# Retention and a mixture of adapters: all attention in 64-token steps on four 64x64 array tiles, in a fixed order

## The chip, the cores and the metric

The kernel runs on one core of a Trainium2 chip. The metric is the device time of one execution in microseconds, as the median of several runs; lower is better. The engines are named as in the profile: PE is TensorE (matmuls), PEld its weight loads, DVE VectorE, ACT ScalarE, POOL GpSimd, SP SyncE (here only a queue that issues DMAs). A line number such as L291 is a line of the kernel before; lines of the kernel after are given where a step has no counterpart.

## The reference

Eight batches of eight heads, 576 tokens, 64 values a head. Scores q k^T are scaled, multiplied by a causal decay gamma_h^(i-j), and applied to v. The result, 512 values a token, goes through a mixture of adapters: eight gates, the best two by a softmax, each adapter of rank 16, and the input added.

```python
scores = scale * np.matmul(q, k.transpose(0, 1, 3, 2))
gamma = 1.0 - 2.0 ** (-5.0 - np.arange(H, dtype=np.float32))
Dmat = np.where(rel >= 0, gamma[:, None, None] ** rel[None, :, :], 0.0)
ret = scores * Dmat[None, :, :, :]
x = np.matmul(ret, v)                       # then as (tokens, 512)
logits = x @ w_gate                         # 8 gates, best 2, softmax weights w
delta[mask] += w[mask, k, None] * ((x[mask] @ A[e]) @ B[e])
out = x + delta
```

All inputs and outputs are fp32.

## The kernel before, in words

**Tiling.** The 576 tokens are four chunks of 128 and a half chunk of 64. A unit is one chunk of two batches (a pair); there are 16 full units and four half units (64 tokens of two batches, stacked on the 128 partitions). Loads go by quads: one chunk of four batches, 1 MB each for q, k and v, into three rotating buffers a tensor; a quad serves two units. The first quad is loaded in two halves.

**The decay** is split: gamma^i goes into q when its transpose is evicted (L241, with aqp), gamma^-j into v on POOL (L197, in place). What earlier chunks contribute is a state P a head and pair, 64x64: chunk by chunk k^T v is added (L387) and POOL multiplies the sum by gamma^128 (L388).

**Stages of one unit.** T (L229): PE transposes q and k, 128x64 outputs; DVE evicts q (L241), ACT k (L250). S (L291): scores, 16 matmuls with 64 rows, 128 stationary columns and 128 moving columns; DVE masks them with the triangle into rt (L302). O: the state part P^T q into px (L359, 16 matmuls on 64x64 tiles with 128 columns, from chunk 1 on) and the state update k^T v into pu (L373, 16). R (L408): the masked part, v^T rt, 16 matmuls with 128 rows, accumulated on px; ACT copies px to xT (L417). Z (L447): xT against adapters A and gates, 128x136 columns; the routing on DVE and ACT (lg L460, m L462, ns L463, sg L468, cm L473, zc L479). B (L512): xT transposed back into po; X (L493): zc transposed, zT by ACT (L498); Y (L533): zT against B, added in po; ACT copies po to osb (L543); a store of each batch on SP (L548). An fp32 matmul is recorded as two passes, each with a weight load.

**The order** is written as a loop over units, one unit after the other, with the next unit's transposes and the previous unit's Y inside it (lines 561 to 576); the framework's scheduler may still move instructions. Eight PSUM banks rotate under one tag. A quad's loads are issued two quads ahead (L562). Half units use 64x64 tiles for scores (L291 with 64 columns, four tiles), the state part (L341, two tiles) and the masked part (L426).

```python
for t in range(NU):
    if t % 2 == 0:
        issue(t // 2 + 2)
    stage_S(t)
    ...
    stage_O(t)
    stage_R(t)
    ...
    stage_T(t + 1)
    stage_B(t - 1); stage_X(t - 1)
    stage_Z(t)
    stage_Y(t - 1)
```

Of the kernel before, what the change touches and what calls it, by code (L numbers as in the profile page):

```python
# [14 lines left out]
AFT = mybir.ActivationFunctionType  # L15


@with_exitstack
def kernel(
# [10 lines left out]
    nc = tc.nc  # L30
# [6 lines left out]
    NP = B // 2  # L37
    NFULL = S // 128
    LH = S - 128 * NFULL
    QUAD = 4  # L40
    NQ = B // QUAD

    scale = 1.0 / float(np.sqrt(Dh))
    gam = 1.0 - 2.0 ** (-5.0 - np.arange(H, dtype=np.float64))
    jj = np.arange(128, dtype=np.float64)

    ident32_np = np.eye(128, dtype=np.float32)
    tri_np = (jj[None, :] >= jj[:, None]).astype(np.float32)
    j64 = np.arange(128) % 64
    i64 = np.arange(64)  # L50
    trih_np = (i64[None, :] >= j64[:, None]).astype(np.float32)
    aqp_np = np.zeros((128, HP, 128), dtype=np.float32)
    g128_np = np.zeros((128, HP), dtype=np.float32)
    for hp in range(HP):
        for ho in range(2):
            g = gam[2 * hp + ho]
            aqp_np[64 * ho : 64 * ho + 64, hp, :] = scale * g ** jj[None, :]
            g128_np[64 * ho : 64 * ho + 64, hp] = g**128.0
    gv_np = np.stack([gam[h] ** (-jj) for h in range(H)], axis=1).astype(np.float32)
    gvh_np = np.stack([gam[h] ** (-j64.astype(np.float64)) for h in range(H)], axis=1).astype(  # L60
        np.float32
    )
    i64_np = np.concatenate([np.eye(64), np.eye(64)], axis=0).astype(np.float32)
    first_np = i64_np
    rest_np = np.concatenate(
        [ident32_np, tri_np, trih_np, gv_np, gvh_np, g128_np], axis=1
    ).astype(np.float32)
    NPK = rest_np.shape[1]
    dr_first = nc.inline_tensor(first_np, "c_first")
    dr_rest = nc.inline_tensor(rest_np, "c_rest")  # L70
    dr_aqp = nc.inline_tensor(aqp_np, "c_aqp")
# [4 lines left out]
    mo = ctx.enter_context(tc.tile_pool(name="moe", bufs=3))  # L76
    pp = ctx.enter_context(tc.tile_pool(name="pp", bufs=8, space=bass.MemoryType.PSUM))

    id64 = cpool.tile([128, 64], FP32, tag="id64", name="id64")
    nc.sync.dma_start(out=id64, in_=dr_first.ap())  # L80
    warm = cpool.tile([128, 1], FP32, tag="warm", name="warm")
    nc.vector.memset(warm, 0.0)
    nc.scalar.activation(out=warm, in_=warm, func=AFT.Sigmoid)
    pack = cpool.tile([128, NPK], FP32, tag="pack", name="pack")
    aqp = cpool.tile([128, HP, 128], FP32, tag="aqp", name="aqp")
    ident32 = pack[:, 0:128]
    tri = pack[:, 128:256]
    trih = pack[:, 256:320]
    gv = pack[:, 320 : 320 + H]
    gvh = pack[:, 320 + H : 320 + 2 * H]  # L90
    g128 = pack[:, 320 + 2 * H : 320 + 2 * H + HP]

    AW = []
    for par in range(2):
        AW.append(cpool.tile([128, HP, ER + E], FP32, tag=f"AW{par}", name=f"AW{par}"))
    Bcat = cpool.tile([128, Dm], FP16, tag="Bcat", name="Bcat")
    ident16 = cpool.tile([128, 128], FP16, tag="ident16", name="ident16")

    def load_moe():
        for dt in range(HP):  # L100
            nc.sync.dma_start(  # L101
                out=AW[0][:, dt, 0:ER].rearrange("p (e r) -> p e r", e=E),
                in_=moe_A[:, 128 * dt : 128 * dt + 128, :].rearrange("e d r -> d e r"),
            )
        nc.sync.dma_start(
            out=AW[0][:, :, ER : ER + E],
            in_=moe_w_gate.rearrange("(t p) e -> p t e", p=128),
        )
        nc.gpsimd.dma_start(out=Bcat, in_=moe_B.rearrange("e r d -> (e r) d"))


    nat = {}

    def issue_full(c, qd, split):
        tiles = []
        for src, tag in ((q, "q32"), (k, "k32"), (v, "v32")):
            tiles.append((src, iop.tile([128, QUAD * H, Dh], FP32, tag=tag, name=tag)))
        parts = ((0, 2), (2, 4)) if split else ((0, 4),)
        for lo, hi in parts:
            for src, tl in tiles:  # L120
                if split and lo == 0 and src is k:
                    nc.sync.dma_start(out=aqp, in_=dr_aqp.ap())
                if split and lo == 0 and src is v:
                    nc.sync.dma_start(out=pack, in_=dr_rest.ap())
                if split and lo == 2 and src is q:
                    load_moe()
                nc.sync.dma_start(  # L127
                    out=tl[:, lo * H : hi * H, :],
                    in_=src[
                        QUAD * qd + lo : QUAD * qd + hi, :, 128 * c : 128 * c + 128, :  # L130
                    ].rearrange("b h j d -> j (b h) d"),
                )
        for half in range(2):
            nat[(c, 2 * qd + half)] = [
                tl[:, half * 2 * H : half * 2 * H + 2 * H, :] for _, tl in tiles
            ]

    def issue_half(qd):

        s0 = 128 * NFULL  # L140
        tiles = []
        for src, tag in ((q, "q32"), (k, "k32"), (v, "v32")):
            tiles.append((src, iop.tile([128, QUAD * H, Dh], FP32, tag=tag, name=tag)))
        for slot in range(2):
            for src, tl in tiles:
                for par in range(2):
                    b = QUAD * qd + 2 * slot + par
                    nc.sync.dma_start(
                        out=tl[64 * par : 64 * par + LH, slot * H : slot * H + H, :],
                        in_=src[b, :, s0 : s0 + LH, :].rearrange("h j d -> j h d"),  # L150
                    )
            nat[(NFULL, 2 * qd + slot)] = [
                tl[:, slot * H : slot * H + H, :] for _, tl in tiles
            ]

    quads = [(c, qd) for c in range(NFULL + 1) for qd in range(NQ)]

    def issue(n):
        if n < len(quads):
            c, qd = quads[n]  # L160
            if c < NFULL:
                issue_full(c, qd, n == 0)
            else:
                issue_half(qd)

    issue(0)

    issue(1)
    nc.vector.tensor_copy(out=ident16, in_=ident32)
    gdec = cpool.tile([128, HP, 2, Dh], FP32, tag="gdec", name="gdec")  # L170
    nc.gpsimd.tensor_copy(
        out=gdec.rearrange("p a b d -> p a (b d)"),
        in_=g128.unsqueeze(2).broadcast_to((128, HP, 2 * Dh)),
    )
    P = [
        cpool.tile([128, HP, 2, Dh], FP32, tag=f"P{bp}", name=f"P{bp}")
        for bp in range(NP)
    ]

    def swap_aw():  # L180
        for ho in range(2):
            nc.gpsimd.tensor_copy(
                out=AW[1][64 * ho : 64 * ho + 64],
                in_=AW[0][64 - 64 * ho : 128 - 64 * ho],
            )

    units = [(c, 2 * qd + s) for c, qd in quads for s in range(2)]
    st = {}
# [131 lines left out]
    def col(full, b, ho):  # L320
        return (ho ^ b) if full else ho
# [289 lines left out]
```

## Time and profile before

| | |
|---|---|
| Median of 3 runs | 207.31 us (205.72 to 207.71) |
| Span of the profiled execution, first to last instruction | 205.1 us |
| The profiled execution's own time beyond its span | not recorded; the runs lie 0.7 to 2.7 us above the span |
| PE busy / weight loads | 183.8 us (90%) / 166.2 us (81%) |
| DVE, ACT, POOL busy | 108.7, 76.6, 59.6 us |
| HBM read, written | 29.32 MB, 9.44 MB |
| Share of the 16 DMA engines (main queue) | 68.0% |

Busy shares are averages over a start that waits for loads, a long even middle and a short tail. The granted PE clock is full from the start's end on. In the groups a line such as "x512 | 34.6, 288" gives the count, the busy microseconds together and the mean nanoseconds of one; what follows is the engine's idle time before them and what ended it. "64*128" in a matmul's row is its tile of the array, rows by columns. In the chain of waits each piece has its start, its length and what it is.

### The profile page before, as it was taken

Reading aid. Unit: us, or ns where it says so; the run is one execution under the profiler, and the core shown is the slowest. Engines: PE = TensorE matmul, PEld = TensorE weight load, DVE = VectorE, ACT = ScalarE, POOL = GpSimd, SP = SyncE. Lnnn points to the kernel's source line nnn. Section 1 sums busy time; section 2 is a strip of 40 time slices with the busy share of each in tenths; the row PEclk is TensorE's granted clock in tenths of the full one; section 3 lists DMA queues with packets and bytes.
Section 4 is the critical chain, followed back from the end, with each engine's and each line's share of the span. In section 5 each row is a group of like instructions: output and inputs, shape, how many; then the busy total and the mean of one; then the engine's idle time right before and its main releaser. Section 6 shows DMA issues by size and latency. Waiting matters only on the chain.

```text
span 205.1 us, 8039 instructions
## 1 busy us (share of the span) xinstructions
PE 183.8 (90%) x3564; PEld 166.2 (81%) x3564; DVE 108.7 (53%) x286; ACT 76.6 (37%) x206; POOL 59.6 (29%) x60
## 2 busy tenths in 40 slices
PE   0476989799999999999999999999999999999950
PEld 0376969598999999999999999999999899888830
DVE  0226364937374746465656565656565655456630
ACT  2022324153525262625252525253434344454430
POOL 1144323521818202727202720643222402000000
PEclk9999999999999999999999999999999999999997
DMA  5989999799998988991799969756545311222222
GB/s 114 277 109 246 249 243 280 194 290 290 253 319 245 261 249 274 284 297 36 220 286 254 266 215 293 213 145 179 150 118 158 96 51 60 101 79 76 58 47 61
DMA packets 57442, 39.14 MB, mean 191 GB/s; under 512 B 30912, under 2 KB 52672, under 8 KB 57408
## 3 DMA queue, kind: packets, MB, share of 16 engines
q1 hardware_dynamic: 57264, 38.50, 68.0%
q8 instruction: 28, 0.46, 0.9%
q0 software_dynamic: 144, 0.13, 0.4%
q14 instruction: 6, 0.05, 0.1%
HBM read 29.32 MB, written 9.44 MB: 189 GB/s over the span
## 4 chain that ended last, share of the span: by engine, by line
PE 72%; SPq 9%; DVE 7%; DMA 5%; ACT 3%; issue 1%; ACTq 0%
PE pz L447 16%; PE px L408 12%; PE ps_s L291 12%; PE pu L373 6%; PE px L359 6%; PE pt_q L229 5%; DMA k<-in_k_dram 5%; PE po L512 4%; SPq L127 4%; PE pt_k L229 4%; PE po L533 3%; DVE rt L302 2%; PE px L426 2%; ACT osb L543 2%; SPq L101 2%; PE pzt L493 2%
## 5 line engine op out<-in xcount | busy, mean ns | idle before, releaser
L197 POOL TENSOR_TENSOR v<-v,pack 128x512 f32<-128x512 f32 x36 | 36.6, 1042 | 28.0 <-DMA v<-in_v_dram 28.0
L417 ACT COPY xT<-px 128x512 f32<-128x512 f32 x32 | 18.7, 585 | 66.0 <-PE px L408 66.0
L388 POOL TENSOR_TENSOR P<-pn,gdec 128x512 f32<-128x512 f32 x16 | 20.3, 1271 | 75.3 <-DVE pn L387 58.9
L302 DVE TENSOR_TENSOR rt<-ps_s,pack 128x512 f32<-128x512 f32 x64 | 39.7, 682 | 4.2 <-PE ps_s L291 4.2
L291 PE MATMUL ps_s<-qT,kT 64*128 64x128 f32 (+1 forms) x640 | 37.4, 275 | 1.2 <-ACT kT L250 1.2
L447 PE MATMUL pz<-AW,xT 128*128 128x136 f32 x288 | 37.8, 283 | 0.4 <-ACT zT L498 0.4
L291 PEld LDWEIGHTS ps_s<-qT,kT 64*128 64x128 f32 (+1 forms) x640 | 33.7, 184 | 5.3 <-DVE lg L460 3.4
L241 DVE TENSOR_TENSOR qT<-pt_q,aqp 128x512 f32<-128x512 f32 x32 | 20.6, 686 | 31.1 <-PE pt_q L229 31.1
L408 PE MATMUL px<-rt,v 128*64 128x128 f32 x512 | 34.1, 275 | 1.8 <-DVE rt L302 1.7
L447 PEld LDWEIGHTS pz<-AW,xT 128*128 128x128 f32 x288 | 34.7, 190 | 0.6 <-ACT zT L498 0.5
L543 ACT COPY osb<-po 128x256 f32<-128x256 f32 x72 | 23.1, 375 | 25.8 <-PE po L533 25.8
L408 PEld LDWEIGHTS px<-rt,v 128*64 128x64 f32 x512 | 29.0, 137 | 3.8 <-DVE rt L302 2.5
L250 ACT COPY kT<-pt_k 128x512 f32<-128x512 f32 x32 | 17.2, 589 | 19.2 <-PE pt_k L229 19.2
L460 DVE COPY lg<-pz 128x16 f32<-128x16 f32 (+1 forms) x20 | 3.5, 173 | 35.0 <-PE pz L447 35.0
L229 PE MATMUL pt_q<-id,q 64*128 64x64 f32 x288 | 13.6, 234 | 6.7 <-DMA q<-in_q_dram 6.7
L373 PE MATMUL pu<-v,k 128*64 128x64 f32 x512 | 18.9, 225 | 0.0
L373 PEld LDWEIGHTS pu<-v,k 128*64 128x64 f32 x512 | 16.5, 137 | 2.7 <-issue 2.1
L229 PEld LDWEIGHTS pt_q<-id,q 64*128 64x128 f32 x288 | 10.8, 142 | 9.6 <-issue 9.4
L229 PE MATMUL pt_k<-id,k 64*128 64x64 f32 x288 | 12.8, 228 | 3.4 <-DMA k<-in_k_dram 3.4
L473 DVE SCALAR_TENSOR_TENSOR cm<-lg,m,sg 128x8 f32<-128x8 f32 x36 | 9.9, 294 | 8.8 <-ACT sg L468 8.8
L229 PEld LDWEIGHTS pt_k<-id,k 64*128 64x128 f32 x288 | 10.9, 143 | 3.8 <-issue 1.7
L359 PE MATMUL px<-qT,P 64*64 64x128 f32 x384 | 13.2, 275 | 0.0
(34 smaller groups left out, 139.9 us busy)
## 6 DMA issues: line engine op xcount, KB each, us to landing
out_dram<-osb SPq DMA_DIRECT2D x32, 256.0 KB, 3.2
q<-in_q_dram SPq DMA_DIRECT2D x2, 512.0 KB, 5.0
k<-in_k_dram SPq DMA_DIRECT2D x2, 512.0 KB, 6.0
v<-in_v_dram SPq DMA_DIRECT2D x2, 512.0 KB, 5.4
q<-in_q_dram SPq DMA_DIRECT2D x8, 128.0 KB, 3.4
k<-in_k_dram SPq DMA_DIRECT2D x8, 128.0 KB, 3.3
v<-in_v_dram SPq DMA_DIRECT2D x8, 128.0 KB, 4.1
out_dram<-osb SPq DMA_DIRECT2D x8, 128.0 KB, 2.4
```

The costliest lines, as they stand in the source:

```text
L197: nc.gpsimd.tensor_tensor(out=v32[:, b * H : b * H + H, :], in0=v32[:, b * H : b * H + H, :], in1=g.unsqueeze(2).broadcast_to((128, H, Dh) ...
L229: nc.tensor.matmul(ps[r][:, hp, b, :] if full else ps[r][:, hp, :], lhsT=src[sl, b * H + 2 * hp : b * H + 2 * hp + 2, :], rhs=id64[sl, :], ...
L241: nc.vector.tensor_tensor(out=o, in0=ps[r], in1=aqp[:, :, 64 * r : 64 * r + 64] .unsqueeze(2) .broadcast_to((128, HP, 2, 64)), op=ALU.mult,)
L291: nc.tensor.matmul(o, lhsT=kT[sl, hp, b, :], rhs=qT[sl, hp, b, :], start=(a == 0 and (b == 0 or not full)), stop=True, skip_group_check=True,)
L302: nc.vector.tensor_tensor(out=r.rearrange("p a b i -> p (a b) i"), in0=ps[ho].rearrange("p a b i -> p (a b) i"), in1=tri.unsqueeze(1).broa ...
L359: nc.tensor.matmul(px[b][64 * cc : 64 * cc + 64, hp, :], lhsT=P[bp][64 * ho : 64 * ho + 64, hp, b, :], rhs=qT[64 * ho : 64 * ho + 64, hp, ...
L373: nc.tensor.matmul(pu[64 * ho : 64 * ho + 64, hp, b, :], lhsT=s["k"][:, b * H + h, :], rhs=s["v"][:, b * H + h, :], start=(hp == 0 and b = ...
L388: nc.gpsimd.tensor_tensor(out=pf, in0=pn, in1=gdec.rearrange("p a b d -> p (a b d)"), op=ALU.mult,)
L408: nc.tensor.matmul(px[b][64 * cc : 64 * cc + 64, hp, :], lhsT=s["v"][:, b * H + h, :], rhs=rt[h][:, b, :], start=(c == 0 and hp == 0), sto ...
L417: nc.scalar.copy(out=xt, in_=px[b])
L447: nc.tensor.matmul(pz[:, b, :], lhsT=xts[b][:, dt, :], rhs=AW[b][:, dt, :], start=(dt == 0), stop=(dt == HP - 1), skip_group_check=True,)
L543: nc.scalar.copy(out=osb[:, b, :, cc ^ b, :], in_=po[cc][:, b])
```

## The change

Both kernels compute the same. In the changed one:

- **Attention in 64-token steps.** The 128 tokens of a chunk are two halves r, which lie on the two partition halves. Scores (S_mm), state update (U_mm), state part (P_mm) and masked part (R_mm) are each 32 matmuls a full unit, with 64 rows, 64 stationary and 64 moving columns, in orders that use the four 64x64 tiles in turn (TILES, FIRST, LAST). The mask is one 64x64 triangle; scores between the halves are not computed, the second half gets the first through the state.
- **Plain-sum state.** q and v are scaled by gamma^pos and gamma^-pos with the position in the whole sequence (scale_nat, on POOL, products of 128x1024, q too and before its transpose). The state is a plain running sum: U_add, two DVE adds a unit, one for each half; P's product with gamma^128 on POOL is gone. Evictions of q become copies (T_out).
- **Half units are doubled**: two units of four batches in place of four of two.
- **A fixed order** (manual_schedule): each engine works in the order of the text, with named banks A to D. A round r holds the state update and scores of unit r+1, state part and masked part of r, transposes of r+2, and B, X, Y of r-1. PE changes tiling three times a round: 64x64 steps, then transposes, then 128x128.
- **turn**: ACT copies one column of px between the state part and each phase of the masked part, which thus waits for it; 16 scores matmuls stand in between. In unit 0 eight matmuls of no use (spacer) stand there.
- **Loads**: the first quad in smaller pieces, k's first two and the adapters' weights on ACT's queue; later quads at the end of every odd round behind a store. One store a unit instead of two. One constant of 208 columns instead of three.

```diff
+TILES = ((0, 0), (1, 1), (0, 1), (1, 0))
+FIRST = ((1, 1), (0, 0), (1, 0), (0, 1))
+LAST = ((1, 1), (0, 0), (0, 1), (1, 0))
...
+    ctx.enter_context(tc.manual_schedule())
...
+    def scale_nat(eng, nm, u, b0=0, b1=2):
+        t = nat[(nm, u)][:, b0 * H : b1 * H, :].rearrange("p (b h) d -> p b h d", h=H)
+        g = (gq if nm == "q" else gv)[:, units[u][0], :]
+        eng.tensor_tensor(
+            out=t,
+            in0=t,
+            in1=g.unsqueeze(1).unsqueeze(3).broadcast_to((128, b1 - b0, H, Dh)),
+            op=ALU.mult,
+        )
...
+    def S_mm(u, hps):
+        s = st[u]
+        for hp in hps:
+            for b in range(2):
+                for ho, r in TILES:
+                    sl = slice(64 * ho, 64 * ho + 64)
+                    mm(
+                        s["ps"][ho][64 * r : 64 * r + 64, hp, b, :],
+                        lhsT=s["kT"][sl, r, hp, b, :],
+                        rhs=s["qT"][sl, r, hp, b, :],
...
+    def U_mm(u):
...
+                for r, ho in TILES:
+                    sl = slice(64 * r, 64 * r + 64)
+                    h = b * H + 2 * hp + ho
+                    mm(
+                        pu[r][64 * ho : 64 * ho + 64, hp, b, :],
+                        lhsT=kn[sl, h, :],
+                        rhs=vn[sl, h, :],
...
+    def P_mm(u):
...
+            for r in range(2):
+                state = s["P0"] if r == 0 else s["P1"]
...
+                for hp in range(HP):
+                    for ho, cc in TILES:
+                        b = ho ^ cc
...
+    def turn(u):
+        t = mo.tile([128, 1], FP32, tag="turn", name="turn")
+        px = st[u]["px"][1]
+        nc.scalar.copy(out=t, in_=px[:, 0, 64:65] if full(u) else px[:, 0, 0, 0:1])
+
+    def R_mm(u, phase):
...
+                for r, cc in (TILES if phase else FIRST if hp + 1 < HP else LAST):
+                    b = r ^ phase
...
-    NU = len(units)
-    stage_T(0)
-    scale_v(0)
-    swap_aw()
-    for t in range(NU):
...
+    for r in range(1, NU):
+        nxt, nn = r + 1, r + 2
+        if nxt < NU and full(nxt):
+            U_open(nxt, ("C0", "C1"))
+            U_mm(nxt)
+        if r > 1:
+            route_a(r - 1)
+            for n in range(2):
+                route_s(r - 1, n)
+        if nxt < NU and full(nxt):
+            U_add(nxt, 0)
+            U_add(nxt, 1)
+        if r > 1:
+            route_b(r - 1)
+        O_open(r, ("A0", "A1"))
+        P_mm(r)
+        turn(r)
+        if nxt < NU:
+            S_open(nxt, ("B0", "B1"))
+            S_mm(nxt, range(0, 2))
+        else:
+            B_mm(r - 1, ("B0", "B1"))
+        R_mm(r, 0)
+        if full(r):
+            turn(r)
+        if nxt < NU:
+            S_mm(nxt, range(2, HP))
+        R_mm(r, 1)
+        if nxt < NU:
+            S_mask(nxt, 0)
+            S_mask(nxt, 1)
+        X_open(r)
+        xT_out(nc.scalar, r, 0)
+        if nn < NU:
+            T_open(nn, "q", ("D0", "D1"))
+            T_mm(nn, "q")
+            T_out(nc.scalar, nn, "q", 0)
+            xT_out(nc.scalar, r, 1)
+            T_open(nn, "k", ("C0", "C1"))
+            T_mm(nn, "k")
+            T_out(nc.vector, nn, "q", 1)
...
+        if nxt < NU:
+            B_mm(r - 1, ("B0", "B1"))
+        X_mm(r - 1, "D0")
+        zT_out(r - 1)
+        Z_open(r, "D1")
+        Z_mm(r, 0)
+        if nn < NU:
+            T_out(nc.scalar, nn, "k", 0)
+            T_out(nc.scalar, nn, "k", 1)
+        Y_mm(r - 1)
+        osb_open(r - 1)
+        osb_out(nc.scalar, r - 1, 0)
+        osb_out(nc.vector, r - 1, 1)
+        Z_mm(r, 1)
+        store(r - 1)
+        if r % 2 == 1:
+            load((r + 1) // 2 + 2, q)
+            load((r + 1) // 2 + 2, k)
+            load((r + 1) // 2 + 2, v)
+        if nn < NU:
+            scale_nat(nc.gpsimd, "v", nn)
+        if r + 3 < NU:
+            scale_nat(nc.gpsimd, "q", r + 3)
```

In the changed kernel's lines, the scores are L198, the state update L225, state and masked part L258 (one helper), the transposes L165, B L443, Z L357, X L425, Y L459, the turn L304, U_add L242 and L244, copies L176 (ACT) and L178 (DVE), the scaling L142.

## The prediction

> **What bounds the kernel now.** First the page: busy shares and the chain that ended last.
>
> ```profile
> span 205.1 us, 8039 instructions
> PE 183.8 (90%) x3564; PEld 166.2 (81%) x3564; DVE 108.7 (53%) x286; ACT 76.6 (37%) x206; POOL 59.6 (29%) x60
> PE 72%; SPq 9%; DVE 7%; DMA 5%; ACT 3%; issue 1%; ACTq 0%
> ```
>
> TensorE is both the busiest engine and the chain. The windows view shows where it has no gap at all, and there DMA is not full:
>
> ```profile
> 65.69:166.53 100.84, 100.84 (x1983) 92.83 (x1982) 59.03 (x151) 41.02 (x111) 33.18 (x31) 1.00 0.72 206
> ```
>
> PE is busy 100.84 of 100.84 us at clock 1.00, DMA share 0.72. One unit of this stretch, from the chain in order of time (start, us, what):
>
> ```profile
> 65.69 1.99 PE ps_s L291 x32
> 67.68 1.03 PE px L359 x32
> 68.71 1.08 PE pu L373 x32
> 69.79 1.75 PE px L408 x32
> 71.54 0.64 PE pt_q L229 x16
> 72.18 0.49 PE pt_k L229 x16
> 72.68 0.49 PE po L512 x16
> 73.17 0.22 PE pzt L493 x2
> 73.39 1.91 PE pz L447 x16
> 75.30 0.44 PE po L533 x4
> ```
>
> Every piece is PE and they add up to 10.04 us. An fp32 matmul is two passes (16 matmuls, x32). Attention proper (the first four) is 5.85 us, the rest 4.19 us. So the change is priced by what it does to PE's round, and then by who can keep up.
>
> **The attention step.** After the change each of scores, state update, state part and masked part is 32 matmuls on 64x64 tiles with 64 columns: 64 passes each, 256 a round instead of 128. Does a pass cost half? The trace has this very form, in the half units, in the timeline:
>
> ```profile
> 176.00 0.56 PEld L291 LDWEIGHTS ps_s<-qT,kT 64*64 64x64 f32 x32 [0.21 <-DVE lg L460]
> 176.47 1.03 PEld L341 LDWEIGHTS pq<-qT,P 64*64 64x64 f32 x32
> ```
>
> L291 uses all four tiles: its 32 weight loads give way to L341's after 0.47 us, 14.7 ns a pass. L341, two tiles only, takes 1.03/32 = 32 ns. L359 (four tiles, 128 columns) takes 1.03/32 = 32 ns, twice the 64-column pace, as it should if the columns set it. I take 14.7, because all the new orders (TILES, FIRST, LAST) alternate the row half and use four tiles in turn: 64 x 14.7 = 0.94 us a step, 3.76 for four, instead of 5.85. The entry into another tiling costs about 0.15 (pt_q 0.64 against pt_k 0.49, same work), paid once for the four steps: 3.91. The lower bound is the same without entry, the upper L341's pace.
>
> [...]
>
> **The rest of PE's round** stays: pt_q, pt_k, po, pzt, pz, po 4.19 us (pz is cut in two around L533, same tiling, nothing added). Two turns: ACT copies one column of px before the masked part may write that bank, so PE waits for the last pass to drain, the copy, and a semaphore. The nearest row for the copy, and the length of one 64-column pass:
>
> ```profile
> L83 ACT ACTIVATE warm<-warm 128x1 f32<-128x1 f32 x1 | 0.2, 203 | 0.0
> L291 PE MATMUL ps_s<-qT,kT 64*64 64x64 f32 x128 | 2.8, 224 | 0.0
> ```
>
> Drain 0.22, copy 0.20, two hops some 0.1: 0.5 to 0.55 us, against 16 scores matmuls in between (32 x 14.7 = 0.47). Left over 0.08 each, taken as 0.1; behind the wait stands all of PE's queue, and on ACT behind the turn the copies of px. Round: 3.91 + 4.19 + 0.2 = 8.3; with 0.05 for the wait below, 8.35 (bounds 8.1 without turns' rest, and 8.8 with an entry paid at each of four steps). In rounds 1 to 3 (chunk 0) the state part is half: 7.9.
>
> **Do the others keep up?** Means of one:
>
> ```profile
> L302 DVE TENSOR_TENSOR rt<-ps_s,pack 128x512 f32<-128x512 f32 x64 | 39.7, 682 | 4.2 <-PE ps_s L291 4.2
> L387 DVE TENSOR_TENSOR pn<-pu,P 128x512 f32<-128x512 f32 x12 | 8.3, 691 | 2.9 <-PE pu L373 2.9
> L417 ACT COPY xT<-px 128x512 f32<-128x512 f32 x32 | 18.7, 585 | 66.0 <-PE px L408 66.0
> L498 ACT COPY zT<-pzt 128x256 f16<-128x256 f16 x16 | 6.2, 390 | 0.0
> L468 ACT ACTIVATE sg<-lg,ns 128x8 f32<-128x8 f32 x36 | 9.2, 303 | 2.9 <-DVE ns L463 2.9
> L197 POOL TENSOR_TENSOR v<-v,pack 128x512 f32<-128x512 f32 x36 | 36.6, 1042 | 28.0 <-DMA v<-in_v_dram 28.0
> ```
>
> ACT: six 128x512 copies 3.5, zT 0.4, two sigmoids 0.6, two turns 0.4: 4.9 of 8.35. DVE: two masks, two adds, two copies at 0.69 are 4.1, the routing chain about 1.4: 5.5. POOL loses P's decay and gains q's scaling: two 128x1024 products a round, at 2 x 1.04 each 4.2 us. Walked through the fixed orders from the round's start: ns ends at 0.8, sigmoids at 1.45 (state update and state part cover them until 2.0), adds 1.2 to 2.6, cm and zc to 3.4, masks (scores end at 3.5) 3.8 to 5.15; then L443 needs the bank that the masks free: PE is there at 5.15. So DVE is just in time, and what delays it by 1 us delays PE by nearly 1 us. ACT also stands before a turn with its sigmoids: a late ns holds the masked part.
>
> **What makes DVE late: POOL.** The timeline, start and duration:
>
> ```profile
> 34.34 4.04 POOL L197 TENSOR_TENSOR v<-v,pack 128x512 f32<-128x512 f32 x4 [4.62 <-DMA v<-in_v_dram]
> 34.35 1.04 DVE L463 SCALAR_TENSOR_TENSOR ns<-m 128x2 f32<-128x2 f32 x1
> 35.77 1.64 DVE L473 SCALAR_TENSOR_TENSOR cm<-lg,m,sg 128x8 f32<-128x8 f32 x2 [0.37 <-ACT sg L468]
> 175.68 0.17 DVE L460 COPY lg<-pz 128x16 f32<-128x16 f32 x1 [2.11 <-PE pz L447]
> 175.88 0.24 DVE L462 MAX8 m<-lg 128x8 f32<-128x8 f32 x2
> 176.16 0.16 DVE L463 SCALAR_TENSOR_TENSOR ns<-m 128x2 f32<-128x2 f32 x1
> 176.77 0.41 DVE L473 SCALAR_TENSOR_TENSOR cm<-lg,m,sg 128x8 f32<-128x8 f32 x2 [0.46 <-ACT sg L468]
> 177.10 0.48 DVE L479 TENSOR_TENSOR zc<-pz,cm 128x128 f16<-128x128 f32 x2
> ```
>
> Beside POOL's products ns takes 1.04 us instead of 0.16 and the cm pair 1.64 instead of 0.41: each waits until the product under way ends, and only these, since L302 beside POOL keeps its 0.68. The products will be twice as long, so a hold is up to 2.1 us. [...]
>
> When does POOL work? Loads of a quad are issued at the end of an odd round; their time to landing now, between 60 and 120 us:
>
> ```profile
> out_dram<-osb SPq DMA_DIRECT2D x14, 256.0 KB, 4.0
> q<-in_q_dram SPq DMA_DIRECT2D x4, 0.2 KB, 6.7
> v<-in_v_dram SPq DMA_DIRECT2D x3, 0.2 KB, 9.6
> ```
>
> ```profile
> 34.20:65.69 31.49, 29.98 (x533) 26.81 (x532) 19.26 (x47) 12.44 (x34) 15.64 (x15) 1.00 0.90 265
> ```
>
> The last row is a stretch in which DMA was full: 265 GB/s at share 0.90. On SP q, k and v stand behind a store of 0.5 MB that waits for the round's output copies; their buffers are free by then, so nothing else holds them. 3.5 MB, or 4.0 with the next store, at 265 GB/s take 13.2 to 15.1 us, so v lands some 13 to 16 us after the round's end; then POOL runs v, q, v back to back for 6.2 us. That is over the start of the second round after (16.7 us), where ns (17.3) and cm (19) stand. Walking landings of 11, 12.5, 14.5, 15.5 and 16.5 us gives holds of 0, 1.4, 1.7, 2.8 and 3.4 us per quad. I take 1.7 for each of quads 3 to 7, 8.5 in all, and 2.2 for round 2 (quad 2's v comes then): 10.7, bounds 0 and 21.
>
> **Start and end.** Two rows of the timeline and one of the chain:
>
> ```profile
> 7.69 4.37 SPq L101 DMA_DIRECT2D AW<-in_moe_A_dram  x4
> 34.20 2.06 PE L291 MATMUL ps_s<-qT,kT 64*128 64x128 f32 x32
> 195.68 1.17 PE pz L447 x8
> ```
>
> Now unit 2's scores start at 34.20, right when quad 1's v lands (POOL's wait for it ends at 34.34). Before that DMA is full:
>
> ```profile
> 0.00:34.20 34.20, 22.62 (x342) 20.19 (x342) 12.46 (x29) 7.92 (x16) 9.46 (x14) 1.00 0.92 213
> ```
>
> The change drops some 0.35 MB of constants ahead of it (aqp, the larger pack): 0.35/0.213 = 1.6 us earlier, 32.7. But round 1 begins with unit 2's state update, which needs v scaled, 2.1 us: 34.8, and PE's whole queue stands behind. The smaller first loads, unit 0's split transposes and the spacers only fill time in which that load is late anyway; so does ACT's new issue of the adapters' loads (4.37 us on SP now) ahead of its first copies of k: unit 0's scores then begin near 10 us, and units 0 and 1 need some 20 us. If they needed more, round 1 would start later by as much.
>
> Rounds 1 to 14: 34.8 + 3 x 7.9 + 11 x 8.35 = 150.4. Round 15 has no state update, 7.4. The two double half units are rounds of 6.9 (no transposes of q and k, pz in column halves at the same pace, 0.7 us wait for xT) and 6.8. The tail repeats the present one, last pz (ends 196.85) to 205.1 = 8.2, plus 0.8 for longer output copies: 9.0. Sum 150.4 + 21.1 + 9.0 = 180.5; with holds 10.7, **191.2 us span against 205.1**. The profile gives no time of its own beyond its span; the median of the runs shown is 207.31, 2.2 more, which I add: **193.4 us**.
>
> DMA as a limit: three loads of 1 MB and two stores a pair of rounds, 4.2 MB in 16.7 us = 251 GB/s, just under those 265: enough, without reserve.
>
> **Rivals.** (1) POOL and DVE do not meet: v lands early or late enough, holds near 0, 183 us. For it: away from the products ns keeps its 0.16; against: products twice as long, on POOL half of every round. (2) The pair meets at its worst, or DMA sinks below 251 GB/s, and each quad costs 3.4 us plus 0.3 a round: 204 to 207. (3) **Slower:** four-tile passes do not keep 14.7 ns in runs of 256, because the trace has it for 32 only, which a filled queue may hide. Place: each round's attention steps. Price per nanosecond: 4,352 passes in all, 4.4 us. From 18 ns on nothing is gained; at 20 ns the time is 216, at L341's 32 ns 269. [...] Against it: L359's passes, four tiles too, follow the scores without a gap (65.69 + 1.99 = 67.68). (4) The change does not do what it says: if bank waits keep the four steps apart, each pays its own entry, 3 x 0.15 a round, 200.
>
> **How the numbers follow.** Forecast (187 to 199) 0.46; rival 1 0.19; rival 2 0.13; rival 4 0.10; rival 3 0.12, of which a quarter stays near no change. Rival 2 lies by a third within 1% of now (205.2 to 209.4, about what this kernel's runs, 205.72 to 207.71, can tell). Faster 0.82, same 0.08, slower 0.10. The range 181 to 207 leaves out the slow side of rival 3 and a little below rival 1.
>
> **What would show it.** Right: L198 x1152, L225 x1024 and L258 x2176, each step of 64 passes about 0.94 us in the chain; rounds of 8.3 us where POOL rests; ns and cm of 1 to 2 us beside 128x1024 products; PE idle under 5% between 35 and 160 us; scores of unit 2 near 36.5. Wrong: passes at 18 ns or more, turns that cost PE over 0.3 us each, q or k transposes waiting for DMA after 50 us, or a round 1 that starts later than 37.

## The result and the profile after

The changed kernel takes 254.34 us (median of 4 runs, 252.25 to 255.96) against 207.31: 1.226 times the time before, 95% interval 1.216 to 1.236. The forecast was 193.4, and its range ended at 207. The profiled execution spans 249.7 us at a mean granted TensorE clock of 0.897. Executions of one kernel differ in the granted clock, so the times of the experiments are medians of the faster ones (within 1.5% of a kernel's fastest), and the profiles of e1, e5, e6 and e11, which are of slower ones, are read for waits and shapes alone.

The page of the changed kernel, the lines that answer to those of before: span, busy shares, the granted clock in 40 slices, the main and the instruction queue, and the shares of the chain.

```profile
span 249.7 us, 12237 instructions
PE 175.2 (70%) x5684; PEld 161.3 (65%) x5684; DVE 106.1 (42%) x260; ACT 78.8 (32%) x200; POOL 69.9 (28%) x46
...
PEclk9999775589979859997999979997999997999995
...
q1 hardware_dynamic: 49728, 37.33, 68.6%
...
q8 instruction: 44, 0.72, 1.3%
...
PE 60%; issue 18%; DMA 9%; SPq 5%; DVE 4%; POOL 1%; ACT 1%; DVEq 0%; ACTq 0%
```

The instruction queue before the change:

```profile
q8 instruction: 28, 0.46, 0.9%
```

TensorE was busy 183.8 us before and is busy 175.2 now, 8.6 us less although the clock is lower (0.897 against 0.995); what grew is its idle time, from 21 us to 75. The chain names the new piece: "issue", time in which TensorE waited for nothing that the profile shows, 18% of 249.7 or 45 us, 1% before. The view of TensorE's waits says where (microseconds in total, times, longest):

```profile
PE px L258 <- issue: 25.5, 11, 6.1
PE ps_s L198 <- issue: 10.0, 5, 2.8
...
PE pu L225 <- issue: 2.8, 2, 1.8
PE pt_k L165 <- issue: 2.5, 2, 1.6
...
PE px L258 <- ACT turn L304: 2.2, 2, 1.3
```

The turns, which the change adds, cost TensorE 2.2 us in this view. The gaps without a cause stand in the attention steps. The chain in order of time shows a round with one of them (start, length, what; an x64 is a whole step of 64 passes):

```profile
104.72 1.09 PE pu L225 x64
105.81 0.93 PE px L258 x64
106.75 0.47 PE ps_s L198 x32
...
108.24 3.66 issue
111.90 0.69 PE px L258 x29
112.60 0.73 PE pt_q L165 x16
113.33 0.85 PE pt_k L165 x16
...
115.36 1.56 PE pz L357 x8
```

The steps go at the pace of the forecast: 0.93 us for 64 passes, 0.47 for 32, 1.09 with the entry into the tiling. Then TensorE stands for 3.66 us in the middle of a step, between two matmuls of one line. And behind the stop the granted clock is lower: 0.50 from 113.0 to 116.4 us, and there pt_k takes 0.85 us instead of 0.50, pz 1.56 instead of 0.98. Of the nine gaps of over 2.3 us after 30 us, seven have such a stretch at half the clock, which begins in the gap or within 1.1 us of its end.

The single records show a rhythm. These are TensorE's gaps of over 0.6 us in this stretch, each with the number of the instruction that it follows (weight loads and matmuls counted together), and the packets of queue q8, which carries 16,384 bytes of instructions in each (start in us, what):

```
108.11 gap 3.79 us after instruction 4508 (L258 to L258)
109.01   instruction packet, 1.31 us long
117.81   instruction packet, 1.28 us long
118.58 gap 2.05 us after instruction 4758 (L225 to L225)
122.00   instruction packet, 1.26 us long
122.50 gap 2.13 us after instruction 5014 (L198 to L198)
```

The gaps come 250 and 256 instructions apart and end 1.4 to 1.6 us after a packet has come. It is so in the whole trace: from 26 to 216 us 24 of the 26 gaps of over 0.8 us lie one, two or three times 250 to 256 instructions behind the one before. 44 packets for 11,368 TensorE instructions are 258 each. Before, 28 packets served 7,128, 255 each, and TensorE had no gap in its even middle: 390 instructions in a round of 10.04 us are 6.6 us a packet. Now a round issues 650, and in the attention steps 256 of them last 1.9 us.

**Theory A**: TensorE waits for its own instructions, which come through the DMA engines in blocks of 256, one block ahead. **B**: four small tiles in turn, or the new order, are slow in themselves. **C**: late data, or GpSimd's products that hold VectorE. A fourth came up in the traces, **D**: the loads themselves became slower. The mean packet of 1024 bytes takes 59 ns in the DMA records of before and 79 in those of after. Median time from issue to landing of a load of 1 MB of v, before and after (the groups of DMA issues, one row of each kernel):

```profile
v<-in_v_dram SPq DMA_DIRECT2D x7, 0.2 KB, 9.3
```

```profile
v<-in_v_dram SPq DMA_DIRECT2D x7, 0.2 KB, 12.6
```

The shape of the loads, their size and their queue are unchanged. What differs is in the compiled programs: the tiles of q, k and v start at addresses that are 0 modulo 64 bytes before and 32 modulo 64 after, because the constants ahead of them have other sizes. The start of round 1 in the chain after the change:

```profile
36.94 1.91 POOL v L142
...
38.89 1.99 PE pu L225 x64
```

### The profile page after: what moved, and what is told of

It reads as the page before. It is cut to its first block, busy times and chain, and to the rows that moved or that the text cites. A ratio compares the mean times of both kernels' runs of the same rounds, so it can differ in the third digit from the quotient of the medians.

```text
span 249.7 us, 12237 instructions
## 1 busy us (share of the span) xinstructions
PE 175.2 (70%) x5684; PEld 161.3 (65%) x5684; DVE 106.1 (42%) x260; ACT 78.8 (32%) x200; POOL 69.9 (28%) x46
## 3 DMA queue, kind: packets, MB, share of 16 engines
q1 hardware_dynamic: 49728, 37.33, 68.6%
## 4 chain that ended last, share of the span: by engine, by line
PE 60%; issue 18%; DMA 9%; SPq 5%; DVE 4%; POOL 1%; ACT 1%; DVEq 0%; ACTq 0%
PE px L258 15%; PE pz L357 13%; DMA v<-in_v_dram 9%; PE ps_s L198 7%; PE pu L225 6%; PE pt_q L165 5%; PE po L443 4%; PE pt_k L165 4%; SPq L119 3%; PE po L459 3%; PE pzt L425 2%; SPq L530 2%; DVE ns L393 1%; PE pz L367 1%; DVE osb L178 1%
## 5 line engine op out<-in xcount | busy, mean ns | idle before, releaser
L142 POOL TENSOR_TENSOR v<-v,pack 128x1024 f32<-128x1024 f32 x18 | 34.3, 1903 | 72.4 <-DMA v<-in_v_dram 72.4
L142 POOL TENSOR_TENSOR q<-q,pack 128x1024 f32<-128x1024 f32 (+1 forms) x18 | 33.4, 1854 | 74.6 <-DMA q<-in_q_dram 69.2
L258 PE MATMUL px<-rt,v 64*64 64x64 f32 x1152 | 30.8, 244 | 25.2 <-issue 22.9
L258 PEld LDWEIGHTS px<-rt,v 64*64 64x64 f32 x1152 | 25.5, 154 | 24.7 <-issue 21.7
L357 PE MATMUL pz<-AW,xT 128*128 128x136 f32 x256 | 38.5, 295 | 1.9 <-POOL AW L601 1.2
L198 PE MATMUL ps_s<-qT,kT 64*64 64x64 f32 x1152 | 30.4, 248 | 10.0 <-issue 10.0
L357 PEld LDWEIGHTS pz<-AW,xT 128*128 128x128 f32 x256 | 34.2, 201 | 2.8 <-POOL AW L601 1.4
L198 PEld LDWEIGHTS ps_s<-qT,kT 64*64 64x64 f32 x1152 | 26.6, 162 | 13.2 <-issue 13.0
L178 DVE COPY osb<-po 128x512 f32<-128x512 f32 (+1 forms) x20 | 13.8, 691 | 44.9 <-PE po L459 41.5
L176 ACT COPY xT<-px 128x512 f32<-128x512 f32 (+1 forms) x35 | 19.6, 565 | 35.8 <-PE px L258 35.8
L225 PE MATMUL pu<-v,k 64*64 64x64 f32 x1024 | 21.5, 237 | 8.2 <-POOL v L142 5.4
L225 PEld LDWEIGHTS pu<-v,k 64*64 64x64 f32 x1024 | 19.0, 150 | 10.5 <-POOL v L142 5.5
L304 ACT COPY turn<-px 128x1 f32<-128x1 f32 x34 | 5.4, 159 | 62.5 <-PE px L258 62.4
L165 PE MATMUL pt_q<-pack,q 64*128 64x64 f32 x288 | 16.0, 255 | 11.6 <-DVE q L142 7.1
L244 DVE TENSOR_TENSOR P<-pu,P 128x512 f32<-128x512 f32 x28 | 19.4, 692 | 8.1 <-PE pu L225 6.3
L176 ACT COPY kT<-pt_k 128x512 f32<-128x512 f32 (+1 forms) x37 | 19.2, 575 | 9.6 <-DMA AW<-in_moe_A_dram 9.0
L258 PE MATMUL px<-qT,P 64*64 64x64 f32 x1024 | 19.6, 223 | 3.4 <-issue 2.6
L178 DVE COPY qT<-pt_q 128x512 f32<-128x512 f32 (+1 forms) x20 | 12.5, 635 | 21.7 <-PE pt_q L165 21.7
L165 PEld LDWEIGHTS pt_q<-pack,q 64*128 64x128 f32 x288 | 12.7, 160 | 13.4 <-DVE q L142 7.1
L258 PEld LDWEIGHTS px<-qT,P 64*64 64x64 f32 x1024 | 17.6, 138 | 4.2 <-issue 2.9
```

What stands on the lines that cost most here:

```text
L142: eng.tensor_tensor(out=t, in0=t, in1=g.unsqueeze(1).unsqueeze(3).broadcast_to((128, b1 - b0, H, Dh)), op=ALU.mult,)
L165: mm(ps[r][:, hp, b, :], lhsT=src[sl, b * H + 2 * hp : b * H + 2 * hp + 2, :], rhs=id64[sl, :], is_transpose=True, start=True, stop=True,)
L176: nc.scalar.copy(out=out, in_=in_)
L178: eng.tensor_copy(out=out, in_=in_)
L198: mm(s["ps"][ho][64 * r : 64 * r + 64, hp, b, :], lhsT=s["kT"][sl, r, hp, b, :], rhs=s["qT"][sl, r, hp, b, :], start=(hp == 0 and b == 0), ...
L225: mm(pu[r][64 * ho : 64 * ho + 64, hp, b, :], lhsT=kn[sl, h, :], rhs=vn[sl, h, :], start=(hp == 0 and b == 0), stop=True, skip_group_check ...
```

## The experiments

**e1: the same columns in half the instructions.** In each of the four steps two matmuls are merged into one of 128 moving columns (here the state update; the other three alike):

```diff
-            for b in range(2):
+            for b in range(1):
...
-                        pu[r][64 * ho : 64 * ho + 64, hp, b, :],
+                        pu[r][64 * ho : 64 * ho + 64, hp, 0:2, :],
```

> The attention matmuls of the changed kernel are merged two by two: 128 moving columns under one stationary operand, so the same columns pass through the same four tiles in the same orders with half the instructions (256 instead of 512 a round, TensorE 3,500 matmuls instead of 5,684). It leaves out the right operand of every second one (one batch's or head's keys, values or state serve two, and one state serves both token halves), so its times are those of the same columns with fewer instructions. Theory A (TensorE waits for its instructions: after every 256 of them it stands until the next block has come by DMA, and a block takes some 4 us or more): the idle time put down to 'issue' in the attention lines goes from 36 us to under 4, the granted clock goes from 0.90 to over 0.97, and the time is 185 to 205. Theory B (four 64x64 tiles in turn, or the fixed order, are slow in themselves): as many columns in the same order, so 240 to 255. Theory C (data that comes late, products of GpSimd that hold VectorE): 240 to 255 as well, with the idle time put down to DMA and DVE.

204.4 us (203.73 and 205.12), and with the gaps 50 us are gone. Of the 45 us of "issue" less than 6 are left, the most here:

```profile
PE px L258 <- issue: 3.8, 3, 2.1
```

A round without a hold, in the chain, goes from 119.35 to 127.46, 8.11 us; the forecast said 8.3:

```profile
119.35 1.03 PE pu L225 x32
120.38 0.87 PE px L258 x32
121.26 0.44 PE ps_s L198 x16
...
127.46 1.03 PE pu L225 x32
```

As many columns pass through the same tiles in the same order, so B falls for passes of equal columns. But 204 is at A's upper edge and the clock was 0.94, not 0.97: something else is left.

**e2: more instructions in the kernel before.**

```diff
-                            o, lhsT=kT[sl, hp, b, :], rhs=qT[sl, hp, b, :],
+                        for i in range(2 if full else 1):
+                            w = slice(64 * i, 64 * i + 64)
+                            o[:, w], lhsT=kT[sl, hp, b, :], rhs=qT[sl, hp, b, w],
```

> The kernel before with nothing changed but that the scores and the state part of full units are issued as two matmuls of 64 columns instead of one of 128: the same tiles, order and columns, and 896 matmuls more (4,460 instead of 3,564), some 520 TensorE instructions (loads and matmuls) in a round of 10 us instead of 390. Theory A: 256 instructions now last 5 us instead of 6.5, just above the 4 us of an unloaded block fetch and below what a fetch takes behind loads of data; so gaps put down to 'issue' appear where none were, 5 to 25 us of them, and the time is 212 to 235. Theory B for the tiles (two tiles of 64 rows at 64 columns run at 32 ns a pass either way) and theory C: no new idle time, 205 to 211.

234.33 us, ratio 1.124 (1.115 to 1.132): the time that A named, but by luck, and not by A. There are next to no gaps of "issue" (0.5 us); the scores themselves became longer. One round's piece in the chain:

```profile
155.40 3.77 PE ps_s L293 x64
159.17 1.23 PE px L363 x61
```

64 passes of 64 columns with 128 stationary columns take 3.77 us, 59 ns each, where 32 of 128 columns took 1.99, 62 ns each: in this form a pass costs nearly the same with 64 columns as with 128, so twice the passes cost nearly twice the time. What sets the 59 ns is left open; each pass also loads 128 stationary columns anew (L293 has 1,152 weight loads for its 1,152 matmuls). A round is now 12.0 us for some 520 instructions, so a block of 256 lasts 5.9 us, and that next to no gaps come there says no more of A than that 5.9 us are enough.

**e3: the changed kernel without loads after the third quad.**

```diff
+        if n > 2:
+            return
```

> The changed kernel without the loads of q, k and v from quad 3 on (and without the scaling that follows them in place: it goes to a scratch tile): the tiles of quads 0 to 2 are used again, so the output is that of other tokens from there. 15 MB of DMA traffic are gone, instruction fetches and stores are left, and every matmul stays. Theory A: the gaps of 'issue' stay, for there are as many instructions, but each is no longer than the bare fetch makes it (about 4 us a block against 1.9 to 2.6 us that 256 instructions last): rounds of 9.3 to 10.5 us, 205 to 232 in all. Theory C (late data, a full DMA): rounds of 8.3, 190 to 200. Theory B: 240 or more.

224.78 us (224.52 to 225.81). The gaps stay with a DMA share of 0.21 from 40 us on, 25 us of them, and none is longer than 2.4 us (6.1 in the changed kernel). So the loads make the gaps longer, but they don't make them. C as the main cause falls.

**e5: 32 bytes.**

```diff
-    warm = cpool.tile([128, 1], FP32, tag="warm", name="warm")
+    warm = cpool.tile([128, 16], FP32, tag="warm", name="warm")
```

> The changed kernel with one constant tile (warm, one column) made sixteen columns wide, so that every tile behind it starts 32 bytes later. In the kernel before the tiles of q, k and v start at addresses that are 0 modulo 64 bytes, in the changed kernel at 32 modulo 64; and there the 1024-byte packets of their loads take 79 ns on average (median 81) against 59 (median 54) before, though loads, sizes and queue are the same. Theory D (the start address makes the loads slow): packets of 54 to 60 ns, v of quad 1 lands near 33 instead of 36.9, round 1 starts near 35 instead of 38.9, and the fetches of instructions find a less busy DMA, so some of the gaps shrink: 236 to 248. Theory A alone (instruction fetches, and the loads slow for another reason): packets as they were, 252 to 256.

233.61 us (233.15 to 234.61): 20.7 us from a constant tile that became wider, a little more than D's range of 236 to 248 allowed. The main queue's 49,728 packets, as many as in the changed kernel, keep the 16 DMA engines busy for 132 us (56.1% of the span of 235.1) instead of 171 (68.6% of 249.7). The groups of DMA issues and the chain:

```profile
v<-in_v_dram SPq DMA_DIRECT2D x7, 0.2 KB, 9.1
```

```profile
22.21 9.38 DMA v<-in_v_dram
31.66 1.91 POOL v L142
33.61 1.98 PE pu L225 x64
```

Quad 1's v lands at 31.66 instead of 36.94, and round 1 starts at 33.61 instead of 38.89. (The expectation's 33 and 35 were a microsecond too late.)

**e12: the reverse, in the kernel before.** The same line there moves q, k and v from 0 to 32 modulo 64.

> The kernel before with its warm tile sixteen columns wide: here the 32 bytes move the tiles of q, k and v from 0 to 32 modulo 64, the reverse of e5. Theory D: 1024-byte packets of some 80 ns instead of 58, the start later by some 4 us, and, as DMA needs 0.72 to 0.9 of its time now, loads that come late in the rounds: 211 to 225. If the address does not matter and something else in e5 did it, 206 to 209.

212.55 us, ratio 1.032 (1.024 to 1.041); quad 1's v lands at 38.46 us instead of 34.34, and the main queue's 57,264 packets, as many as before, keep the 16 engines busy for 171 us (81.4% of 209.6) instead of 139 (68.0% of 205.1). The main queue's share and the row of v:

```profile
q1 hardware_dynamic: 57264, 38.50, 81.4%
```

```profile
v<-in_v_dram SPq DMA_DIRECT2D x7, 0.2 KB, 12.3
```

The two runs together show D, in both directions. The line moves every tile behind it by 32 bytes; that the tiles of the loads are the ones that count is read from their times to landing (v: 12.6 and 12.3 us at 32 modulo 64, 9.3 and 9.1 at 0). The tiles that the stores read, osb, speak for it too: in the compiled programs they start at 32 modulo 64 before and at 0 in e12, and it is the slower one.

**e6: both mended**, the merged pairs of e1 with the line of e5.

> The merged pairs of e1 (same columns, half the attention instructions, wrong operands for every second one as there) with the same 32 bytes of shift. Theory A with D: no gaps of 'issue', the start 4 us earlier, the loads as fast as before the change: what is left is the forecast's own sum, 190 to 199. Theory A without D: 203 to 208, as e1. If holds of VectorE by GpSimd's products are what keeps e1 at 206 rather than the loads, 200 to 206.

191.37 us (190.24 to 192.92), ratio 0.922 (0.913 to 0.931). The forecast was 193.4: with the instructions halved and the addresses put back, its sum comes out within 2 us. In part that is luck, for two misses cancel: rounds without a hold are shorter than the 8.35 of the sum (8.11 in e1), and the clock is 0.955 to 0.971 instead of 1.00. TensorE's largest wait, in a profiled execution of 204.03 us, and one of its places in the chain:

```profile
PE pt_q L165 <- DVE zc L428: 12.0, 5, 2.9
```

```profile
101.39 3.25 DVE cm L423 x2
```

It is the hold of VectorE by GpSimd: beside products of 1.90 us the pair of cm takes 3.25 us instead of the 0.41 that it takes without. It comes in five rounds, two pairs of neighbours and one alone.

**e10: the holds.** e6 with each of GpSimd's products cut in two.

```diff
+        if b1 - b0 == 2:
+            scale_nat(eng, nm, u, 0, 1)
+            scale_nat(eng, nm, u, 1, 2)
+            return
```

> The merged pairs with the shift (e6, 192 us; wrong operands for every second one as there), with each product of GpSimd cut into two of 128x512, about 1.04 us each instead of 1.9. If holds of VectorE by products under way are what is left of the rounds, each hold is at most one short product, and about half of the forecast's 10.7 us comes back: 184 to 189. If POOL's total time or the load's landing decides (v scaled too late), 190 to 194.

187.47 us (186.71 to 188.28), 3.9 us less; the wait in its trace:

```profile
PE pt_q L169 <- DVE zc L432: 4.6, 8, 1.1
```

**e11: one step merged only**, with the line of e5.

```diff
-            for b in range(2):
+            for b in range(1):
                 for r, ho in TILES:
```

> The changed kernel with the shift, and only the state update merged in pairs (the values of one batch under the keys of the other are left wrong; same columns): some 585 instructions a round instead of 650 (e5, 234.6 us) or 390 (e6, 192.2). Theory A: a block of 256 costs 3.5 us at least and 4 or more beside loads, so a round costs 2.29 blocks, 8.0 to 9.2 us, instead of 2.54 and 8.9 to 10.2: 212 to 226, between the two in proportion to the instructions (221). If some step alone (the update, or another) caused the gaps, 234 or 192.

223.1 us (222.52 and 223.73). From e5 to e11 512 matmuls less, 1,024 instructions, give 10.5 us, 10.2 ns an instruction; from e11 to e6 1,600 matmuls less, 3,200 instructions, give 31.8 us, 9.9 ns. The price goes with the number of instructions and not with a step.

**e7: the price by itself.** Three runs of 1,024 passes behind the end of the changed kernel, DMA idle.

```diff
+    for cols in (16, 64, 128):
+        for n in range(128):
+            for r, cc in TILES:
+                mm(ps[r][64 * cc : 64 * cc + 64, n % 2, 0:cols], lhsT=id64[sl, :], rhs=pack[sl, 0:cols], ...)
```

> The changed kernel with three runs of matmuls behind its last output, which need no data and write nothing that is read: 512 matmuls on four 64x64 tiles in turn with 16 columns, then 512 with 64, then 512 with 128 (1,024 passes, 2,048 TensorE instructions, 8 blocks of 256 each). No data is loaded meanwhile. Theory A: the runs of 16 and of 64 columns take the same time, 8 blocks at 3.4 to 4.2 us, 27 to 34 us, in bursts with gaps of 1 to 2 us after every 256 instructions; the run of 128 columns goes at its 32 ns a pass, 33 us, without gaps. Theory B (the tiles set the pace in long runs): one steady pace in each, longer for 64 columns than for 16. The forecast's own pace (14.7 ns a pass at 64 columns however long the run): 15 us for 64 columns.

The runs lie at about 245 to 274, 274 to 303 and 303 to 332 us: 29 us each, 16, 64 and 128 columns alike. In the chain the middle one is regular (128 passes are 256 instructions), and the last one has next to no gaps:

```profile
280.78 2.09 PE run L726 x128
282.87 1.38 issue
284.25 2.09 PE run L726 x128
286.34 1.38 issue
...
324.58 3.72 PE run L726 x128
328.30 0.02 issue
```

With next to nothing else on the DMA engines a block costs 3.47 us at least: 2.09 at work and 1.38 waiting at 64 columns (other gaps of this run are up to 1.92), 3.72 and next to no wait at 128 columns, which last longer than the fetch. The look-ahead of one block in theory A fits the DMA records of the changed kernel: two blocks begin behind gaps at 120.63 and 124.63 us, instruction packets start 1.4 and 1.1 us later (122.00 and 125.76), and behind the next gaps TensorE goes on 1.4 and 1.5 us after the packets' ends. From gap to gap they are 4.0 and 3.6 us long; the 4 us a block of the expectations of e1, e2, e3 and e8 were an estimate. The run of 16 columns had few gaps, unlike the expectation: it went at a granted clock of 0.50, and its blocks took 3.61 us by themselves; why the clock was low there, without long gaps, is not shown. The windows view (last columns: granted clock, DMA share, GB/s):

```profile
246.00:272.00 26.00, 25.36 (x928) 24.98 (x924) 0.00 (x0) 0.00 (x0) 0.00 (x0) 0.50 0.10 25
275.00:302.00 27.00, 17.65 (x975) 16.45 (x968) 0.00 (x0) 0.00 (x0) 0.00 (x0) 0.94 0.02 4
```

**e9: the same at 64 columns, beside loads** that last until about 265 us, with the line of e5.

```diff
+    for i in range(9):
+        nc.sync.dma_start(out=tl, in_=src[...])     # 1 MB each
```

> The changed kernel with the 32 bytes of shift, and behind its last output nine loads of 1 MB (q, k and v again, into the same buffers; nothing reads them) beside 1,024 matmuls on four 64x64 tiles in turn with 64 columns (2,048 passes, 16 blocks of 256 instructions). The loads last some 35 to 40 us, the run longer, so its first part runs beside a full DMA and its last part beside an idle one. Without loads a block was 2.09 us of work and 1.38 of standing still. Theory A as far as it says that blocks come through the DMA engines: the gaps are 2.5 to 6 us beside the loads and go back to 1.4 us after them. If TensorE stands every 256 instructions for a reason of its own, 1.4 us throughout.

```profile
241.50 2.09 PE run L733 x128
243.59 1.91 issue
245.50 2.09 PE run L733 x128
247.59 3.83 issue
...
267.44 2.09 PE run L733 x128
269.54 1.38 issue
```

A gap is 1.9 to 3.8 us beside the loads and 1.4 to 1.6 behind them; beside the loads there are also three blocks at a lower clock, of 2.7 to 3.7 us of work, with gaps of 0.2 to 1.3. So a fetch takes longer beside loads, though the usual price of company, half a microsecond, is less than I had expected (gaps of 2.5 to 6). Whether the two meet in the DMA engines or in the memory is not shown.

**e8: one part of the change alone**, the scores on four tiles in the kernel before.

```diff
+                        for ho, r in ((0, 0), (1, 1), (0, 1), (1, 0)):
+                            ps[ho][64 * r : 64 * r + 64, a, b, 64 * r :],
+                            lhsT=kT[sl, hp, b, 64 * r : 64 * r + 64], rhs=qT[sl, hp, b, 64 * r :],
```

> The kernel before with one part of the change alone: the scores of full units on four 64x64 tiles, the first key half against all 128 queries and the second only against the second query half, 32 matmuls in place of 16; the masked tiles are kept and their unused block is zero from the start, and VectorE masks in two parts of 256 elements. The output is the reference's. By the four-tile passes (32 of 128 columns at 32 ns, 32 of 64 at 14.7) scores take 1.5 us instead of 1.99, 1.65 with an entry into the tiling: 0.35 to 0.5 us less in 16 rounds of 10.04. TensorE instructions are some 455 a round, 256 in 5.4 us, above the 4 us that an unloaded fetch takes. Theory A: few gaps, 198 to 207. Theory B: 208 to 220.

208.16 us (206.81 to 209.72), ratio 1.005 (1.000 to 1.010): nothing gained, and a time in B's range. Its waits put 0.4 us down to "issue", so gaps are not the reason. The step in the chain:

```profile
107.34 1.78 PE ps_s L310 x50
```

With the last passes the step ends at 109.25, 1.9 us instead of the 1.5 expected (some records are missing, 64 passes were issued): about 30 ns a pass, near the 32 ns of 128 columns, although half the passes have 64. So B holds for passes of unequal columns; that the tiles with 128 columns hold the others up, because the tiles take turns, is argued from this pace alone. The 0.1 us that is left is lost elsewhere in the round: the masked part behind VectorE's masks, which are now in two pieces, takes 1.87 us here instead of 1.75. An earlier form of this edit (e4), which left the block of scores that is not computed unwritten, gave no time.

**e13: a version that computes the reference's output.** The line of e5, the products of e10, and every second full unit from unit 2 on in one step of 128 tokens as before the change.

```diff
+    def whole(u):
+        return full(u) and u >= 2 and u % 2 == 0
...
+        if nxt < NU and whole(nxt):
+            SW_mask(nxt, 0)
+            SW_open(nxt, 1, Y)
+            SW_mm(nxt, 1)
```

> A version that computes the reference's output: the changed kernel with the 32 bytes of shift and the products of GpSimd cut in two, in which every second full unit from unit 2 on (7 of 16) does its attention in one step of 128 tokens, as the kernel before does (scores 1.99 us, state part 1.03, state update 1.08, masked part 1.75, no turns), and the others in steps of 64 tokens. A round then has some 525 TensorE instructions instead of 650, and TensorE's work is 9.0 to 9.3 us instead of 8.3 (10.04 before the change). Theory A: 525 instructions are 2.05 blocks, 7.2 us at 3.5 us a block and 8.6 at 4.2, so few gaps are left: 35 + 15 rounds of 9.2 + 14 for the half units + 9 for the end + some 5 of holds is 201, 2 more outside the span: 197 to 208, against 234.6 for steps of 64 tokens throughout (e5). If blocks beside loads cost 5 us or more, rounds of 10.3: 215 or more.

204.44 us (204.36 to 206.14) against 208.20 beside it, ratio 0.986 (0.979 to 0.994): within what was expected, and ahead of the kernel before by 0.6 to 2.1% only. A gap in the chain is rare now, and TensorE is the chain again:

```profile
PE 77%; DMA 9%; SPq 6%; issue 2%; DVE 2%; POOL 1%; ACT 1%; DVEq 0%; ACTq 0%
```

## Why the prediction was wrong

The chain of runs, from the changed kernel: 254.3; addresses put back (e5) 233.6; one step merged (e11) 223.1; all merged (e6) 191.4; the forecast 193.4. Of the 61 us by which it missed, the supply of instructions is 42 to 50 (e5 to e6, and the changed kernel to e1) and the addresses 13 to 21 (e1 to e6, and the changed kernel to e5). Both were outside its sum. Point by point:

- **The attention step: 64 passes at 14.7 ns, 0.94 us. Right as a pace, wrong as a time; this is the step that failed.** The chain has 0.93, and 1.09 with the entry of 0.15. But the sum took the passes as always there. In long runs they come at 3.47 us for 128 at best, 27 ns a pass, because their instructions, 256 for 128 passes, come no faster (e7).
- **Rival 3** had this place ("do not keep 14.7 ns in runs of 256, because the trace has it for 32 only, which a filled queue may hide") and, at 0.12, too small a chance; its price of 4.4 us a nanosecond gives 247 at 27 ns. The argument against it, that L359's passes follow the scores without a gap, says nothing of supply: a round of the kernel before used 390 instructions in 10 us. The page of before carried the hint, unread: the instruction queue's 28 packets for 7,128 instructions, and an even middle that shows only that 6.6 us a block are enough. The price of a faster stream had no upper bound in that trace. The 27 ns are an average: inside a block the starts lie 16 ns apart (2.09 us for 128), and behind it TensorE stands for 1.38 us (e7).
- **DMA: 251 GB/s needed, 265 to be had. Wrong in the second number.** It was read in a kernel whose buffers start at a multiple of 64 bytes. With buffers at 32 modulo 64 the kernel before moves 225 GB/s (e12, mean of the page's ten slices from 36.7 to 89.1 us, nine of them at a share of 0.9 or more), less than the 251. The sum's start suffers from the same: the bytes ahead of round 1 became fewer as forecast, but from 10 to 36 us only 197 GB/s came, where the forecast took 213.
- **The start: v of quad 1 at 32.7, round 1 at 34.8. Wrong by 4.1 us (38.89); with the addresses put back 31.66 and 33.61, some 1 us earlier than forecast.**
- **Turns, 0.1 each. Near enough**: in e1's round the 16 passes behind a turn take 0.56 us and 16 passes of scores 0.44, so a turn costs 0.12 at most. The 0.1 of its two hops was the author's estimate; around one turn of the changed kernel they are at most 0.12 and 0.05 us (the state part's passes end at 106.75, the copy runs from 106.87 to 107.03, the masked part starts at 107.08).
- **The other rounds' parts and the entry: right.** 8.11 us in e1 for a round without a hold, against 8.3.
- **GpSimd's holds, 10.7 us, bounds 0 to 21: right in kind and about in size.** In the changed kernel the gaps cover most of them; in e6 the wait is 12.0 us in five rounds of an execution of 204.03 us, and products half as long give 3.9 us of the median back. So rival 1 (no holds) falls. Of rival 2 the holds at their worst (3.4 us a quad) did not show, with 2.9 us as the longest wait; its other half, DMA below 251 GB/s, came true by way of the addresses, and these cost 13 to 21 us in all, more than its 0.3 us a round.
- **Clock 1.00, unsaid. Wrong**: 0.897; it is low behind long gaps (0.50 in the round shown above), and with gaps and most of the holds gone it is 0.968 (e10).
- **Rival 4 (bank waits, 200)** did not show; the four steps follow each other.

## What to carry to other kernels

Count TensorE's instructions per microsecond and not only its columns: here, over some 70 instructions a microsecond (256 in 3.5 us, e7), and over 43 to 64 beside loads (256 in 4.0 to 5.9 us, e9), the engine waits for its program, so a split into smaller tiles pays only as long as its instructions stay below that rate. Compare the addresses of the tiles that DMAs write when constants ahead of them change size. A rate taken from the trace of before holds only while what sets it stays in place.

## What was not expected of the hardware

- TensorE's instructions come in blocks of 256 (16,384 bytes) by DMA, and a block takes 3.47 us at least with the DMA engines nearly idle, 4.0 to 5.9 beside loads (e7, e9). Crossing into the next block cost the kernel before no gap in its even middle (6.6 us a block) and costs 1.38 us of every 3.47 in the run of 64 columns (e7).
- Loads into tiles that start at 32 modulo 64 bytes: 79 ns for a 1024-byte packet (after), against 59 at 0 modulo 64 (before), and for a load of 1 MB of v 12.6 and 12.3 us from issue to landing (after, e12) against 9.3, 9.1 and 9.3 (before, e5, e6); that is 5 us of the start (e5), and 5 us (e12) to 21 us (e5) of the time.
- On 64 rows with 128 stationary columns a pass takes 59 ns with 64 columns (e2) and 62 with 128 (before).
- In turns over four tiles, passes of 128 and of 64 columns in equal number take about 30 ns each (e8), near the pace of 128 alone; that the longest of the four sets it is argued from this pace alone.
